# When the first group's twiddled inverse matrices are made, and which other groups are made early, in a Hyena convolution with a gated network behind it

## The chip, the core and the metric

The kernel runs on one core of one Trainium2 chip. The core has a matrix engine (PE; its weight loads are shown as PEld), a vector engine (DVE), a scalar engine (ACT), a general engine (POOL) and a queue that issues transfers (SP). Each engine works through its own instructions in the order in which they were written and waits on semaphores for the others. The metric is the time of one execution in microseconds on the device, as the median of several executions; a lower one is better.

## The reference, cut to what matters

The first part is a long convolution over 12480 positions for 4 batches and 128 channels; the second is a network with a cosine gate that is applied to every position.

```python
B, S, D = x.shape                                   # 4, 12480, 128
h_mlp = np.maximum(pos_emb @ w1, 0.0) @ w2
window = np.exp(-0.01 * np.arange(S))[:, None]
h_filt = h_mlp * window
u = x * v
Uf = np.fft.rfft(u, n=2 * S, axis=1)
Hf = np.fft.rfft(h_filt, n=2 * S, axis=0)
y = np.fft.irfft(Uf * Hf[None], n=2 * S, axis=1)[:, :S]
z = (x * y).reshape(B * S, D)                       # 49920 tokens

h = z @ w_in                                        # d_ff = 2048
out = (h * np.cos(h)) @ w_out
```

## The kernel before, in words

The Fourier transforms are written as matrix products over two factors, 96 and 120. A batch goes through five steps. `u_units` loads x and v, multiplies them and folds the product into the large tile `slots`. `f1_units` and `f2_units` are the two steps of the forward transform, and `f2_units` multiplies by the filter's transform. `i1_units` is the third transform step, the first of the inverse one: 64 pairs of channels, each with four matmuls (L476), one ACT copy (`other`, L484) and two DVE instructions (L486) that write `slots` back. `i2_units` is the last step: 30 groups of four output columns each. For a group, PE multiplies `slots` by four matrices (L501, in two halves of eight instructions), DVE multiplies the result by x (L506, `zs`), and the rows go to the DRAM tensor `zd`, from which the network reads them.

The four matrices of a group lie in a tile `tm` and depend only on the column. `make_t` makes one out of two tables, `rows` and `tw_t`. It calls `turn`, which has two forms: one ACT instruction (L291) and one DVE instruction (L293); or, given a spare tile, two ACT instructions (L291, L296) and one POOL instruction (L297). `make_group` makes the four of a group and stores them in the DRAM tensor `td` (L651). When it is called with `summed` equal to G, which is 4, all four take the second form; with G // 2, the first and third take the first form. Batches 1 to 3 load every group's matrices from `td` (L670).

For batch 0 there are two sorts of groups. Those in `SOME` are made ahead by `some_groups`, within the third step of batch 0, and loaded from `td` in the last step like those of the other batches. The others are made in the last step itself, each while the group before it is multiplied: `before(j)` in `i2_units` returns the generator of `make_group`, and `units` takes one matrix of it at a time.

`units` is the frame of all steps. It first calls `before` for the tiles that are needed at once, ahead of its first `yield`, and then hands out its work in parts, each with a price in `yield`. The network's loop asks for such parts after each of its 16 chunks of a block (`owed`), so that convolution and network are interleaved on PE in a fixed order. In batch 0 a group of the last step costs 3.5 chunks (`FIRST_STEPS`), and `inverse_units` draws the loads and products of batch 1 (`u_units`) beside it.

All of this begins after the third step of batch 0, which runs without the network. Beside its 64 pairs, `beside` draws two other generators: every 14th part, a piece of `convert_units`, which turns the network's output weights from 64-bit to 32-bit words (DVE L151, L133, L141; POOL L135, L137, L147, L156; ACT L144, L146); and every fifth other part, a step of `some_groups`. There are 24 such steps, one matrix each. What is left of either generator runs at the end of the step. As its last act, `some_groups` advances `backs[0]`, the inverse units of batch 0: that opens the pool of the last step, issues the load of x for group 0 (`xs`) and makes group 0's four matrices.

In the network, a chunk is a matmul (L737), an ACT instruction (L740), a DVE rounding (L743), a POOL subtraction (L746), an ACT sine (L751), a DVE product (L753) and a second matmul (L762). Four PSUM tiles hold the results of L737 and of the transposes.

Of the kernel before, what the change touches and what calls it, by code (L numbers as in the profile page):

```python
# [30 lines left out]
def kernel(  # L31
# [68 lines left out]
    G = BANK // D  # L100
    UA = 2
    NG = N2 // G
# [262 lines left out]
    def n2s(g):  # L365

        a = g * UA
        return [*range(a, a + UA), *range(N2 - UA - a, N2 - a)]

    def load_pairs(t, src, b, first, second):  # L370

        start = src[b, first:first + UA, :]
        nc.sync.dma_start(t[:, :, :], bass.AP(
            tensor=start.tensor, offset=start.offset,
            ap=[[N2 * D, R], [(second - first) * D, 2], [1, UA * D]]))
# [114 lines left out]
    def i2_mm(ps, t, g, part):  # L490
        for i in range(part * G // 2, (part + 1) * G // 2):
            n2 = n2s(g)[i]
            a = abs(n2 - MID) if n2 >= H else n2 + 1
            if a % H == 0:
                places = a, N2 + a
            elif n2 < H:
                places = a, N2 + H + a
            else:
                places = H + a, N2 + a
            for r, place in enumerate(places):  # L500
                nc.tensor.matmul(ps[0:R, i * D:(i + 1) * D], t[:, i, r, :],  # L501
                                 slots[0:N1, :, place, :], start=(r == 0), stop=(r == 1))

    def i2_out(pool, ps, xs, b, g):
        zs = pool.tile([R, 2, UA, D], F32, name="zs")
        nc.vector.tensor_tensor(  # L506
            zs[:, :, :, :].rearrange("p h n d -> p (h n d)"), ps[0:R, :],
            xs[:, :, :].rearrange("p h n -> p (h n)"), op=ALU.mult)
        z = zs[:, :, :, :].rearrange("p h n d -> p (h n) d")
        row = (b * NG + g) * R  # L510
        if row > 0:
            nc.sync.dma_start(zd[row:row + R, :, :], z)
        else:
            zbs[0] = z
        made[0] += 1
        yield
# [7 lines left out]
    def units(n, steps, before, mm, after, parts, ahead=2):  # L524


        for j in range(min(ahead, n)):
            for _ in before(j) or ():
                pass
        yield 0.0  # L530
        last = iter(())
        for j in range(n):
            early = iter(before(j + ahead) or () if j + ahead < n else ())
            now = None
            for i in range(parts):
                if i == 0 or 2 * i == max(parts, 2):
                    now = mm(j, now, min(i, 1))
                if i == 0 and parts == 1:
                    now = mm(j, now, 1)
                next(last, None)  # L540
                next(early, None)
                yield steps / parts
            for _ in early:
                pass
            next(last, None)
            last = after(j, now)
        for _ in last:
            pass
        yield REST

    SOME = range(2, NG, 5)
    REST = 3.0
    U_STEPS, F1_STEPS, F2_STEPS, I1_STEPS, I2_STEPS = 2.0, 0.8, 2.9, 0.8, 1.5
    FIRST_STEPS, I2U_STEPS = 3.5, 3.0
# [1 line left out]
    def u_units(b, bufs, u, engine, side="left"):  # L556

        with tc.tile_pool(name="xv", bufs=bufs, side=side) as pool:
            tiles = {}

            def before(j):
                tiles[j] = u_load(pool, bufs, b, j * UA)

            def after(j, _):
                for half in range(2):
                    u_multiply(tiles[j], half, engine(j, half))
                    yield
                if j == H // UA - 2:
                    clear_gap(u)
                u_sums(u, tiles.pop(j), j * UA)  # L570
                yield

            yield from units(H // UA, U_STEPS, before, lambda j, ps, i: None, after, 3,
                             ahead=bufs - 2)

    def f1_units(bank, u, share=0.5, evict=f1_evict):
        def mm(j, ps, i):
            if i == 0:
                ps = bank()
            f1_mm(ps, u, j, i)  # L580
            return ps

        return units(CB, F1_STEPS, lambda j: None, mm, lambda j, ps: evict(ps, j, share), 2)

    def f2_units(bank):
        with tc.tile_pool(name="there", bufs=3) as pool:
            ws, hs = {}, {}

            def before(j):
                ws[j] = pool.tile([KE, 2, N2], F32, name="w")  # L590
                nc.sync.dma_start(ws[j][:, :, :], wd[j, :, :, :])
                hs[j] = pool.tile([N2, 2, CB, 4], F32, name="h")
                nc.sync.dma_start(hs[j][:, :, :, :], hd[j, :, :, :, :])

            def mm(j, ps, i):
                if i == 0:
                    ps = bank()
                f2_mm(ps, ws[j], 2 * j, i)
                return ps

            yield from units(N1 // 2, F2_STEPS, before, mm,
                             lambda j, ps: f2_product(pool, ps, hs.pop(j), 2 * j, False), 4)
# [39 lines left out]
    def make_group(pool, g, t, summed):  # L642

        for i, n2 in enumerate(n2s(g)):
            if summed < G and i % 2 == 0:
                make_t(t[:, i, :, :], n2)
            else:
                spare = pool.tile([N1, 2, R], F32, name="spare", bufs=2)
                make_t(t[:, i, :, :], n2, spare=spare[:, :, :])
            yield  # L650
        nc.sync.dma_start(td[g, :, :, :, :], t[:, :, :, :])  # L651

    def some_groups(pool):
        for g in SOME:
            t = pool.tile([N1, G, 2, R], F32, name="some", bufs=2)
            yield from make_group(pool, g, t, G)
        next(backs[0])

    def i2_units(bank, b, bufs):

        with tc.tile_pool(name="back", bufs=2, side="left" if b else "right") as pool:
            ts, xss = {}, {}

            def before(j):
                ts[j] = pool.tile([N1, G, 2, R], F32, name="tm", bufs=bufs)
                xss[j] = pool.tile([R, 2, UA * D], F32, name="xs", bufs=bufs)
                load_pairs(xss[j], x, b, n2s(j)[0], n2s(j)[UA])
                if b == 0 and j not in SOME:
                    return make_group(pool, j, ts[j], G // 2)
                nc.sync.dma_start(ts[j][:, :, :, :], td[j, :, :, :, :])  # L670

            def mm(j, ps, i):
                if i == 0:
                    ps = bank()
                i2_mm(ps, ts[j], j, i)
                return ps

            yield from units(NG, I2_STEPS, before, mm,
                             lambda j, ps: i2_out(pool, ps, xss.pop(j), b, j),
                             4 if b == 0 else 2, ahead=bufs - 1)  # L680

    def inverse_units(bank, b):

        if b + 1 == B:
            yield from i2_units(bank, b, 3)
            return
        new = u_units(b + 1, 3, slots[0:R, :, :, :],
                      lambda j, half: nc.gpsimd if b == 0 and j % 2 > half else nc.vector,  # L690
                      side="right" if b else "left")
        parts = 4 if b == 0 else 2
        for i, steps in enumerate(i2_units(bank, b, 2)):
            if i > 2 * parts:
                for _ in range(i % parts > 0 if b == 0 else 1 + i % 2):
                    next(new, None)
            yield steps * (FIRST_STEPS if b == 0 else I2U_STEPS) / I2_STEPS
        yield from new
# [95 lines left out]
    with tc.manual_schedule():  # L794
        with tc.tile_pool(name="psum", bufs=8, space=PSUM) as psum, \
                ExitStack() as first:
            def bank():
                return psum.tile([P, BANK], F32, name="ps")
# [67 lines left out]


            backs = [inverse_units(lambda: bank(), b) for b in range(B)]

            def beside(units, pieces, more=lambda pool: iter(())):  # L870
# [28 lines left out]
            nc.vector.memset(quarter[:, :], 0.25)  # L899
            nc.sync.dma_start(w_in_sb[:, :], wind[:, :])  # L900
            beside(i1_units(bank), [(w_out_sb[:, c, :], w) for c, w in out_pieces], some_groups)

        ps_acc = ctx.enter_context(tc.tile_pool(name="ps_acc", bufs=1, space=PSUM))
# [25 lines left out]
        steps = [(n, c) for n in range(NALL) for c in range(NFC)]  # L929
# [57 lines left out]
```

## Time and profile before

| | us |
|---|---|
| median of 4 runs | 3772.33 |
| lowest and highest | 3769.38, 3773.37 |
| the profiled execution | 3773.37 |
| its span, first to last instruction | 3771.6 |
| PE busy | 3694.4 (98%) |
| DVE busy | 2781.5 (74%) |
| ACT busy | 2519.1 (67%) |
| POOL busy | 2573.4 (68%) |

The profile comes from one execution. Its page gives the busy time of each engine and, slice by slice, the share of time it was busy and the clock that PE was granted, where 1.00 is full speed. The chain of work that ended last is followed back from the last instruction, each time to what released the waiting one. A timeline gives start, duration, engine, line, and the tiles written and read; "x4" after a row counts instructions merged into it; in brackets stands how long the engine was idle before, and what ended that. A busy PE is not PE at its peak, because matmuls are pipelined and their ends are modelled.

### The profile page before, as it was taken

How to read it: one execution, taken by the hardware profiler on the slowest of the kernel's cores; microseconds unless marked ns; L12 is line 12 of the kernel's file. 1: busy time of each engine (PE TensorE's matmuls, PEld its weight loads, DVE VectorE, ACT ScalarE, POOL GpSimd, SP SyncE). 2: the span in 40 equal slices, each digit the busy share in tenths (PEclk: the TensorE clock that was granted, in tenths of full speed). 3: DMA queues.
4: the chain of work that ended last, by engine and by line, in shares of the span. 5: the costliest groups of instructions: out<-in, count | busy, mean ns of one | idle time of the engine just before them, and what ended most of it. 6: DMA issues, size and time to landing. Idle time of an engine off the chain costs nothing.

```text
span 3771.6 us, 47191 instructions
## 1 busy us (share of the span) xinstructions
PE 3694.4 (98%) x13546; PEld 2108.3 (56%) x13546; DVE 2781.5 (74%) x5562; ACT 2519.1 (67%) x4683; POOL 2573.4 (68%) x2342
## 2 busy tenths in 40 slices
PE   7898999999999999999999999999999999999999
PEld 6777555655566555555565556555566544444444
DVE  7887887688866777788766786788765566666666
ACT  5757776766665557766655567666664677777777
POOL 7667776588854665688745664788644577777776
PEclk9999999999999999999999999999999999999999
DMA  6263551022202550122103540122105200000000
GB/s 166 63 186 105 150 149 56 18 71 79 74 18 69 178 159 28 33 79 79 57 18 110 177 124 20 49 79 75 41 14 172 82 23 17 17 23 17 17 23 13
DMA packets 209498, 276.14 MB, mean 73 GB/s; under 512 B 17111, under 2 KB 146535, under 8 KB 209111
## 3 DMA queue, kind: packets, MB, share of 16 engines
q1 hardware_dynamic: 209239, 273.12, 24.6%
q8 instruction: 109, 1.79, 0.2%
q14 instruction: 150, 1.23, 0.1%
HBM read 193.64 MB, written 79.42 MB: 72 GB/s over the span
## 4 chain that ended last, share of the span: by engine, by line
PE 86%; DVE 4%; POOL 3%; DMA 3%; ACT 2%; issue 2%; SPq 0%; POOLq 0%; DVEq 0%; ACTq 0%
PE ph L737 33%; PE acc L762 28%; PE cv L501 5%; PE cv L762 5%; PE cv L476 4%; PE cv L404 3%; PE cv L445 3%; PE ph L126 2%; POOL f L746 2%; DMA hd<-h 2%; PE ps L404 1%; DMA tm<-td 1%; ACT cs L751 1%; DVE gt L753 1%; PE ps L476 1%
## 5 line engine op out<-in xcount | busy, mean ns | idle before, releaser
L746 POOL TENSOR_TENSOR f<-a,k 128x512 f32<-128x512 f32 (+1 forms) x1568 | 1989.1, 1269 | 1056.8 <-DVE k L743 1054.2
L737 PE MATMUL ph<-at,w_in_sb 128*128 128x512 f32 (+1 forms) x3136 | 1598.8, 591 | 8.3 <-DVE gt L753 7.5
L740 ACT ACTIVATE a<-ph,quarter 128x512 f32<-128x512 f32 (+1 forms) x1568 | 1072.2, 684 | 678.0 <-PE ph L737 669.3
L762 PE MATMUL acc<-gt,w_out_sb 128*128 128x512 f32 (+1 forms) x2688 | 1369.5, 591 | 0.0
L753 DVE TENSOR_TENSOR gt<-ph,cs 128x512 f32<-128x512 f32 (+1 forms) x1568 | 1077.7, 687 | 371.0 <-ACT cs L751 356.2
L751 ACT ACTIVATE cs<-f 128x512 f32<-128x512 f32 (+1 forms) x1568 | 981.2, 626 | 394.7 <-POOL f L746 392.3
L743 DVE TENSOR_SCALAR k<-a 128x512 f32<-128x512 f32 (+1 forms) x1568 | 798.3, 509 | 541.9 <-ACT a L740 530.2
L762 PEld LDWEIGHTS acc<-gt,w_out_sb 128*128 128x128 f32 x2688 | 508.0, 189 | 642.5 <-issue 631.2
L737 PEld LDWEIGHTS ph<-at,w_in_sb 128*128 128x128 f32 x3136 | 552.2, 190 | 342.8 <-issue 257.9
L471 POOL TENSOR_TENSOR slots<-slots,t 120x256 f32<-120x256 f32 x384 | 311.4, 817 | 61.9 <-DVE t L464 35.1
L501 PEld LDWEIGHTS cv<-slots,tm 96*104 96x104 f32 x1920 | 239.2, 169 | 114.4 <-issue 82.0
L501 PE MATMUL cv<-slots,tm 96*104 96x128 f32 x1920 | 254.7, 274 | 13.6 <-DMA tm<-td 5.2
L762 PE MATMUL cv<-gt,w_out_sb 128*128 128x512 f32 (+1 forms) x448 | 224.5, 583 | 0.7 <-DVE gt L753 0.7
L476 PEld LDWEIGHTS cv<-cs,slots 120*96 120x96 f32 x1536 | 176.7, 167 | 67.6 <-issue 65.5
L476 PE MATMUL cv<-cs,slots 120*96 120x120 f32 x1536 | 183.1, 266 | 0.0
L445 PE MATMUL cv<-slots,w 124*120 124x256 f32 x576 | 173.0, 380 | 0.0
L445 PEld LDWEIGHTS cv<-slots,w 124*120 124x120 f32 x576 | 103.6, 184 | 123.8 <-issue 112.3
L404 PEld LDWEIGHTS cv<-c,slots 104*124 104x124 f32 x768 | 132.5, 192 | 71.3 <-issue 58.3
L404 PE MATMUL cv<-c,slots 104*124 104x192 f32 x768 | 151.2, 326 | 4.9 <-DVE gt L753 3.6
L762 PEld LDWEIGHTS cv<-gt,w_out_sb 128*128 128x128 f32 x448 | 84.9, 190 | 104.5 <-issue 99.5
L392 DVE TENSOR_TENSOR xt<-xt,vt 104x256 f32<-104x256 f32 x177 | 134.3, 762 | 0.3 <-DMA vt<-in_v_dram 0.3
L486 DVE TENSOR_TENSOR slots<-cv,other 96x240 f32<-96x240 f32 x384 | 133.1, 394 | 1.5 <-ACT other L484 1.4
(129 smaller groups left out, 2552.2 us busy)
## 6 DMA issues: line engine op xcount, KB each, us to landing
h<-hd SPq DMA_DIRECT2D x144, 240.0 KB
tm<-td SPq DMA_DIRECT2D x96, 312.0 KB
xt<-in_x_dram SPq DMA_DIRECT2D x120, 208.0 KB
vt<-in_v_dram SPq DMA_DIRECT2D x120, 208.0 KB
xs<-in_x_dram SPq DMA_DIRECT2D x120, 208.0 KB
zd<-zs SPq DMA_DIRECT2D x119, 208.0 KB
zb<-zd SPq DMA_DIRECT2D x96, 256.0 KB
w<-wd SPq DMA_DIRECT2D x144, 116.2 KB
```

Source lines behind the costliest of these rows:

```text
L404: nc.tensor.matmul(ps[0:KE, i * 2 * N1:(i + 1) * 2 * N1], u[:, b, 0:KE, i], c1[0:u.shape[0], :, :].rearrange("p r k -> p (r k)"), start=Tr ...
L445: nc.tensor.matmul(pi, w[:, i, :], parts[0:KE, :, k], start=True, stop=True)
L471: nc.gpsimd.tensor_tensor(y[:, r], y[:, r], t[:, r], op=op)
L476: nc.tensor.matmul(ps[0:N1, (i * 2 + r) * N2:(i * 2 + r + 1) * N2], parts[0:N2, r, :, b, i], cs[:, r, :], start=True, stop=True)
L501: nc.tensor.matmul(ps[0:R, i * D:(i + 1) * D], t[:, i, r, :], slots[0:N1, :, place, :], start=(r == 0), stop=(r == 1))
L737: nc.tensor.matmul(ph[:, 0:m], w_in_sb[:, c * P:(c + 1) * P], ats[n][:, 0:m], start=True, stop=True)
L740: nc.scalar.activation(a[:, 0:m], ph[:, 0:m], AF.Identity, bias=quarter[:, 0:1], scale=INV_TWO_PI)
L743: nc.vector.tensor_scalar(out=k[:, 0:m], in0=a[:, 0:m], scalar1=ROUND, scalar2=ROUND, op0=ALU.add, op1=ALU.subtract)
L746: nc.gpsimd.tensor_tensor(f[:, 0:m], a[:, 0:m], k[:, 0:m], op=ALU.subtract)
L751: nc.scalar.activation(cs[:, 0:m], f[:, 0:m], AF.Sin, scale=TWO_PI)
L753: nc.vector.tensor_tensor(gt[:, 0:m], ph[:, 0:m], cs[:, 0:m], op=ALU.mult)
L762: nc.tensor.matmul(accs[n][:, 0:m], w_out_sb[:, c, :], gt[:, 0:m], start=(c == 0), stop=(c == NFC - 1))
```

## The change

The set `SOME` has a step of 6 instead of 5: groups 2, 8, 14, 20 and 26 are made ahead, where it was 2, 7, 12, 17, 22 and 27. The four matrices of group 0 are made one at a time as steps of `some_groups`, ahead of its last group (26), and no longer in one go behind all of them. For this `units` now yields after each matrix of what it does in advance, `some_groups` advances `backs[0]` G + 1 times, once per step, and `inverse_units` passes the four additional yields of batch 0 through. The last matrix of group 26 is then what runs at the end of the third step.

```diff
         for j in range(min(ahead, n)):
             for _ in before(j) or ():
-                pass
+                yield 0.0
         yield 0.0
...
-    SOME = range(2, NG, 5)
+    SOME = range(2, NG, 6)
...
     def some_groups(pool):
         for g in SOME:
+            if g == SOME[-1]:
+                for _ in range(G + 1):
+                    next(backs[0])
+                    yield
             t = pool.tile([N1, G, 2, R], F32, name="some", bufs=2)
             yield from make_group(pool, g, t, G)
-        next(backs[0])
...
         parts = 4 if b == 0 else 2
-        for i, steps in enumerate(i2_units(bank, b, 2)):
+        back = i2_units(bank, b, 2)
+        for _ in range(0 if b else G):
+            yield next(back)
+        for i, steps in enumerate(back):
             if i > 2 * parts:
```

## The prediction

> **What bounds the kernel now.** I read the page's busy rows first: PE is busy 98% of the span, and its slices leave room only in the first sixth. Three stretches bound the question: the third step with its tail (273.4 to 338.5 us), the first inverse pass beside the network (to 600), and the rest.
>
> ```profile
> 273.40:338.50 65.10, 56.03 (x512) 54.59 (x512) 49.66 (x154) 42.65 (x132) 45.31 (x59) 0.96 0.25 78
> 338.50:600.00 261.50, 247.63 (x965) 141.15 (x966) 224.91 (x363) 188.65 (x378) 197.81 (x197) 0.99 0.50 148
> 600.00:3771.60 3171.60, 3156.79 (x10892) 1720.51 (x10890) 2282.45 (x4446) 2124.33 (x3674) 2144.11 (x1816) 1.00 0.21 62
> ```
>
> The columns are stretch, length, busy time of PE, weight loads, DVE, ACT, POOL, then clock, DMA share, GB/s. From 600 us on PE has 15 us free in 3172, and the change alters no instruction there. A microsecond won or lost before 600 therefore reaches the end whole. Before 600, PE waits about 14 us in the first pass, so that stretch is not PE's alone.
>
> Next, the chain that ended last, at the tail of the third step:
>
> ```profile
> 336.91 0.33 DVE power L151
> 337.24 0.20 DVE slots L486
> 337.48 1.02 DVE slots L486 x3
> 338.50 0.35 DVE tm L293
> 338.86 0.04 issue
> 338.90 3.76 PE cv L501 x16
> 342.68 0.70 DVE zs L506
> ```
>
> The third step ends with the last L486 at 338.50. Of group 0's matrices only the first DVE instruction (L293, 0.35) is on the chain; then come 16 matmuls, 0.235 us each. Are they slow because the other matrices are late? The fine stretches say no:
>
> ```profile
> 336.00:337.00 1.00, 0.00 (x0) 0.00 (x0) 1.00 (x4) 1.00 (x4) 0.08 (x1) 0.83 0.00 0
> 337.00:338.00 1.00, 0.00 (x0) 0.00 (x0) 1.00 (x4) 1.00 (x4) 1.00 (x2) 0.50 0.00 0
> 342.00:343.00 1.00, 1.00 (x7) 1.00 (x6) 0.32 (x1) 0.00 (x0) 0.39 (x1) 0.50 0.73 232
> 344.00:345.00 1.00, 0.41 (x5) 0.21 (x3) 0.00 (x0) 0.51 (x1) 0.00 (x0) 1.00 0.58 155
> ```
>
> PE has nothing to do from 334 on, its granted clock is 0.50 from 337 to 343, and in 342 to 343 it is busy throughout at that clock. The last matrix of group 0 is made by 340.24 (POOL L297, 339.62 plus 0.62), two microseconds before the 16 end. The clock sets their pace.
>
> Then the price of a group made within the first pass. The timeline of L506, one per group, gives the time from group to group; these are groups 10 to 17:
>
> ```profile
> 424.63 0.68 DVE L506 TENSOR_TENSOR zs<-cv,xs 104x512 f32<-104x512 f32 x1
> 431.59 0.68 DVE L506 TENSOR_TENSOR zs<-cv,xs 104x512 f32<-104x512 f32 x1
> 441.22 0.67 DVE L506 TENSOR_TENSOR zs<-cv,xs 104x512 f32<-104x512 f32 x1
> 449.11 0.68 DVE L506 TENSOR_TENSOR zs<-cv,xs 104x512 f32<-104x512 f32 x1
> 458.98 0.68 DVE L506 TENSOR_TENSOR zs<-cv,xs 104x512 f32<-104x512 f32 x1
> 466.95 0.68 DVE L506 TENSOR_TENSOR zs<-cv,xs 104x512 f32<-104x512 f32 x1
> 475.69 0.68 DVE L506 TENSOR_TENSOR zs<-cv,xs 104x512 f32<-104x512 f32 x1
> 483.31 0.68 DVE L506 TENSOR_TENSOR zs<-cv,xs 104x512 f32<-104x512 f32 x1
> ```
>
> Two groups without a loaded one (from 12 to 14) take 17.76, elsewhere in the pass up to 17.84. The pair around the loaded group 12 (424.63 to 441.22) takes 16.59, the pair around 17 (466.95 to 483.31) 16.36. A group that is loaded and not made saves 1.2 to 1.5 us there.
>
> **The change part by part.**
>
> **Other groups kept.** Groups 2, 7, 12, 17, 22, 27 become 2, 8, 14, 20, 26. Group 2 is common. Pair sums over all 30 of L506 give what the old five save against 17.83: 7: 1.32, 12: 1.23, 17: 1.48, 22: 1.25, 27: 1.49, together 6.77. The four new ones are all even, like 12 and 22, so 4 x 1.24 = 4.96. Cost: 6.77 - 4.96 = +1.81 us. Why are the even ones worth less? PE's weight loads wait 2.2 us for the loaded matrices at group 12 and 1.5 at 22, but 0.3 and 0.2 at 17 and 27. Bounds: if the new ones saved as odd ones do (1.48 each), +0.85; if their loads ate the whole saving, +6.8. I take +1.81, since even rows exist. In instructions this is one group more: six ACT (0.45 each), two DVE L293 (median 0.97), two POOL L297 (0.8) and one store on SP, one load of 312 KB less.
>
> **The tail.** Old: six ACT, two DVE, two POOL, a load of xs and a store of td stand between the third step and the first L501. New: the last matrix of group 26 (two ACT, one POOL) and its store, which L501 does not need. DVE loses L293 in front, so PE starts after the last L486, at 338.54 for 338.90: -0.36 us. The 16 matmuls keep 3.76, since PE is idle from 334 to 338.5 still. Bounds: 0, and -2.0 if the clock were full (16 x 0.13 = 2.1 for 3.76, with the 0.36). The load of group 2's matrices (issued 343.83, landed 348.27) meets a freer queue, as xs and one store have gone earlier. That is worth nothing: the network's fourth up-projection waits until 349.4 for the first gate (L753 at 348.79, 0.59), since PSUM holds four of L737's results, and that gate moves only with the start.
>
> **Within the third step.** Of 24 places, 23 still make a matrix and one issues a store alone. Matrices 1 and 3 of group 0 take one ACT instruction and one DVE instruction (L293) where one of another group takes two ACT and a POOL. ACT and POOL have gaps here, so what they save (0.37 of ACT at a place) counts for no more than the DVE gap behind it, 0.21 to 0.25. DVE carries the step: it runs L486 back to back between conversions. So L293's time counts. Undisturbed it is 0.42. But beside POOL it is longer:
>
> ```profile
> 419.12 0.73 POOL L392 TENSOR_TENSOR xt<-xt,vt 104x256 f32<-104x256 f32 x1
> 419.70 1.61 DVE L293 SCALAR_TENSOR_TENSOR tm<-rows,tw_t,tm 96x208 f32<-96x208 f32 x1
> 419.81 1.27 POOL L746 TENSOR_TENSOR f<-a,k 128x512 f32<-128x512 f32 x1
> ```
>
> It ends 0.23 after two POOL instructions that follow without a gap. The L486 rows, which read a matmul's result, keep 0.36 whatever POOL does. By the built order, the first L293 comes behind the third unit after a conversion: 320.5 in old times, with POOL at L147 to 320.73 and L297 behind it without a gap to about 321.3. It ends near 321.55: 1.05, less the DVE gap of 0.21 that it fills, +0.84. The second comes behind the first unit after the next conversion, at 325.91. POOL then runs L137 (325.84 to 326.92), and L147 follows with a gap of 0.07. It ends near 327.16: 1.25, less gaps of 0.25 and 0.21, +0.8. Together +1.6. Bounds: +0.2 (0.42 each, less the gaps) and +2.4 (held through L147 as well, to 327.96). I take +1.6, as the three rows above show both the hold and its end. The place that only stores saves nothing: no DVE gap stands behind it (L486 at 328.34 runs without one until L151 at 330.25).
>
> On SP, the xs load and td store of group 0 move ahead of group 26's store. The conversion's loads are already issued, and the store's wait for POOL holds up only that later store. The two L293 hold L486 and so ACT's next copy of a result, both within the sum above; PE has up to eight banks ahead and no one waits for it.
>
> The rule in the Trainium skill, "SBUF — State Buffer", section "Who interferes with whom", speaks against the move: a DVE instruction with two SBUF inputs contends with a GpSimd one that reads SBUF, and whichever starts later blocks until the other's whole instruction is done. Read as one instruction, it would free the first L293 at the end of L147 (0.47 in all, +0.26) and the second at the end of L137 (+0.8): +1.1. The 1.61 us row shows the hold lasting over two instructions without a gap, which makes +1.6.
>
> **Sum:** +1.81 - 0.36 + 1.6 = +3.05 us against the profiled execution's 3773.37 (span 3771.6, and 1.8 around it), so 3776.4. That execution stands 1.04 above the median of 3772.33; on the median it is 3775.4, +0.08%. What this kernel's measurement can tell from no change is about 0.2%, 7.5 us.
>
> **The rivals.**
>
> **The tail was the point (faster).** L293 is not held, the clock returns early and the new groups save as odd ones: +0.2 - 2.0 + 0.85 = -0.95 us, 3771.4. For it: 7 us of half clock stand there. Against it: PE's idle stretch stays over 4 us. Chance 0.15; even so not faster by 0.2%.
>
> **Loads come late (slower).** In the first pass the even groups' matrices are read soon after the load is issued, and PE waits. The load of group 2 takes 4.43 us from issue to landing. If each of the four waits another 2.2 us (the worst wait seen), the exchange costs 1.81 + 8.8, and the total is +11.9: 3784.2. For it: 2.2 and 1.5 at both even groups. Against it: those waits are already in the 1.24. It passes 7.5 us from 1.1 us more at each of the four. Chance 0.10.
>
> **The hold is longer, or absent.** DVE is held through all of POOL's conversion (+2.4), or not at all (+0.2), the rest as forecast: 3776.2 or 3774.0. Chance 0.25. **The exchange costs nothing**, because other waits fill in: 3773.6. Chance 0.05.
>
> **How the numbers follow.** The forecast itself has 0.45; all but the late loads are within 0.2%. The low end is the first rival less the 2 us by which runs of before scatter; the high end is the largest bound of the exchange with the largest hold, +8.8 us: 3769.5 to 3781. Faster by over 0.2%: 0.03, out of the first rival's 0.15, for a return of the clock that does more than I priced; slower: 0.11, the late loads and 0.01 of the longer hold; within: the other 0.86.
>
> **What would show it.** Right: two L293 of about 1 us within the third step; its last L486 1 to 2 us later; the first L501 directly behind it; clock still 0.50 there; pairs around 7, 12, 17, 22, 27 at 17.8 and around 8, 14, 20, 26 at 16.6; identical durations after 600. Wrong: L293 at 0.42, a full clock at the first L501, or pairs that stay long around the new groups.

## The result, and the profile after

| | before | after |
|---|---|---|
| median of the runs shown, us | 3772.72 (61 runs) | 3776.88 (41 runs) |
| lowest and highest, us | 3769.38, 3777.64 | 3772.14, 3784.19 |
| after by before, with its 95% interval | | 1.0012 [1.0008, 1.0016] |
| the profiled execution, us | 3773.37 | 3780.25 |
| its span, us | 3771.6 | 3778.5 |

The change costs 4.2 us (0.11% of the medians). That is slower, within the 0.2% that the prediction calls no change. The forecast was +3.05 us. The runs scatter over 12 us where those of before scatter over 8, and the profiled execution lies 3.4 us above its own median, so its trace shows more loss than the median has.

I read the same three stretches first (stretch, length, busy time of PE, weight loads, DVE, ACT, POOL, then clock, DMA share, GB/s):

```profile
273.40:338.50 65.10, 55.58 (x508) 54.30 (x507) 51.00 (x155) 42.95 (x131) 43.90 (x56) 0.95 0.26 81
338.50:600.00 261.50, 243.73 (x944) 137.95 (x944) 218.88 (x353) 182.86 (x367) 191.84 (x192) 0.98 0.48 143
600.00:3778.50 3178.50, 3163.18 (x10907) 1723.41 (x10905) 2292.81 (x4453) 2121.95 (x3682) 2149.13 (x1820) 1.00 0.21 62
```

The middle row is the one that moved: PE is busy 243.73 where it was 247.63, and its clock is 0.98 where it was 0.99. To place the loss I measured from event to event, since this execution also reaches the third step 2.6 us earlier, with nothing changed before it:

| stretch, us | before | after | difference |
|---|---|---|---|
| start to the third step's first L476 | 273.42 | 270.80 | -2.62 |
| from there to the first L501 | 65.48 | 65.86 | +0.38 |
| first L501 to the first L506 | 3.78 | 3.75 | -0.03 |
| first L506 to the thirtieth | 243.87 | 252.53 | +8.66 |
| thirtieth L506 to the end | 3185.04 | 3185.54 | +0.50 |

Nearly all of it is in the first inverse pass. The timeline of L506, one row per group, here groups 6 to 8 and 18 to 21:

```profile
387.99 0.67 DVE L506 TENSOR_TENSOR zs<-cv,xs 104x512 f32<-104x512 f32 x1
394.86 0.68 DVE L506 TENSOR_TENSOR zs<-cv,xs 104x512 f32<-104x512 f32 x1
407.06 0.68 DVE L506 TENSOR_TENSOR zs<-cv,xs 104x512 f32<-104x512 f32 x1
...
494.93 0.68 DVE L506 TENSOR_TENSOR zs<-cv,xs 104x512 f32<-104x512 f32 x1
501.88 0.68 DVE L506 TENSOR_TENSOR zs<-cv,xs 104x512 f32<-104x512 f32 x1
515.45 0.67 DVE L506 TENSOR_TENSOR zs<-cv,xs 104x512 f32<-104x512 f32 x1
523.32 0.68 DVE L506 TENSOR_TENSOR zs<-cv,xs 104x512 f32<-104x512 f32 x1
```

The pair around the loaded group 8 (387.99 to 407.06) takes 19.06 and that around 20 (494.93 to 515.45) takes 20.52, where the forecast had 16.6 and a pair without a loaded group takes 17.85. These two loads not only save nothing, they cost. The pairs around 14 and 26 took 16.38 and 17.05. Of the groups that lost their load, 12, 17 and 22 behaved as forecast: the pairs around them took 17.93, 17.85 and 17.76. Groups 7 and 27 now stand beside a loaded one, so their pairs do not show it.

What happens at group 20 is seen on PE's timeline (start, duration, engine, line; in brackets, idle before):

```profile
497.55 1.02 PE L768 MATMUL acc<-gt,w_out_sb 128*128 128x512 f32 x2
501.74 2.01 PE L501 MATMUL cv<-slots,tm 96*104 96x128 f32 x8 [3.16 <-DMA tm<-td]
503.54 1.91 PE L743 MATMUL ph<-at,w_in_sb 128*128 128x512 f32 x2
```

The timeline of the queue SP over the same stretch:

```profile
492.38 0.39 SPq L727 DMA_DIRECT2D zb<-zd  x1
494.42 0.33 SPq L651 DMA_DIRECT2D td<-tm  x1
495.64 0.32 SPq L373 DMA_DIRECT2D xs<-in_x_dram  x1
496.05 0.34 SPq L673 DMA_DIRECT2D tm<-td  x1
```

The load of the group's matrices (L673; L670 before) is issued at 496.05, and PE, which reads it next, starts 5.7 us later, after an idle wait of 3.16. Then the matmuls themselves are slow: two of L743 take 1.91 where two of the same shape (L768) took 1.02. PE's own stretches (length, busy, clock, DMA share, GB/s) show why:

```profile
498.00:501.00 3.00, 0.57 (x2) 1.00 0.79 268
501.00:507.50 6.50, 5.76 (x13) 0.50 0.42 121
507.50:512.00 4.50, 4.50 (x20) 0.97 0.00 0
```

From 501.0 on the granted clock is 0.50, for 6.83 us. In 6.50 us of these PE is busy for 5.76, so a wait of 3.2 us is followed by about 2.9 us of lost matmul time. At group 8 a wait of 2.12 is followed by 3.41 us at 0.50. Before has no half clock between 345 and 600.

The waits of PE and its weight loads in 345 to 600 for loaded matrices (total, times, longest, us), before:

```profile
PEld cv L501 <- DMA tm<-td: 5.1, 5, 2.2
...
PE cv L501 <- DMA tm<-td: 2.6, 2, 1.4
```

After:

```profile
PE cv L501 <- DMA tm<-td: 7.6, 4, 3.2
PEld cv L501 <- DMA tm<-td: 7.1, 4, 3.0
```

In the third step, DVE and POOL around the two L293 of group 0:

```profile
317.35 0.73 POOL L147 TENSOR_TENSOR sig<-sig,low 128x256 f32<-128x256 f32 x1
317.83 0.47 DVE L293 SCALAR_TENSOR_TENSOR tm<-rows,tw_t,tm 96x208 f32<-96x208 f32 x1
318.04 0.76 POOL L297 TENSOR_TENSOR some<-some,spare 96x208 f32<-96x208 f32 x1
...
323.57 1.08 POOL L137 TENSOR_SCALAR power<-power 128x256 uint32<-128x256 uint32 x1
323.61 0.58 DVE L293 SCALAR_TENSOR_TENSOR tm<-rows,tw_t,tm 96x208 f32<-96x208 f32 x1
```

They take 0.47 and 0.58, not 1.05 and 1.25. The first began beside L147 and ended at 318.30, long before L297 did at 318.80. The second ran inside L137 and was not held to its end at 324.65.

Last, the chain at the tail of the third step:

```profile
334.91 0.33 DVE power L151
335.24 1.27 DVE slots L486 x4
336.52 0.14 issue
336.65 4.75 PE cv L501 x24
```

And the fine stretches there (columns as in the first fence):

```profile
336.00:337.00 1.00, 0.35 (x2) 0.38 (x3) 1.00 (x3) 1.00 (x4) 1.00 (x2) 0.50 0.00 0
337.00:338.00 1.00, 1.00 (x6) 1.00 (x6) 0.65 (x2) 1.00 (x4) 0.62 (x1) 0.50 0.27 76
```

L293 is gone from the chain, and the first L501 starts 0.14 after the last L486, where it was 0.40. The clock is still 0.50, for 6.83 us as before.

### The profile page after: what moved, and what is told of

It is laid out like the page before. It is cut to its first block, busy times and chain, and to the rows that moved or that the text cites. A ratio compares the mean times of both kernels' runs of the same rounds, so it can differ in the third digit from the quotient of the medians.

```text
span 3778.5 us, 47191 instructions
## 1 busy us (share of the span) xinstructions
PE 3696.6 (98%) x13546; PEld 2108.2 (56%) x13546; DVE 2786.3 (74%) x5564; ACT 2511.6 (66%) x4681; POOL 2573.1 (68%) x2340
## 4 chain that ended last, share of the span: by engine, by line
PE 86%; POOL 3%; DMA 3%; DVE 3%; ACT 2%; issue 2%; SPq 0%; POOLq 0%; DVEq 0%; ACTq 0%
PE ph L743 33%; PE acc L768 28%; PE cv L501 5%; PE cv L768 5%; PE cv L476 4%; PE cv L445 3%; PE cv L404 3%; PE ph L126 2%; POOL f L752 2%; DMA hd<-h 2%; DMA tm<-td 1%; PE ps L404 1%; PE ps L476 1%; ACT cs L757 1%; DVE slots L486 0%
## 5 line engine op out<-in xcount | busy, mean ns | idle before, releaser
L743 PE MATMUL ph<-at,w_in_sb 128*128 128x512 f32 (+1 forms) x3136 | 1601.0, 592 | 8.5 <-DVE gt L759 7.6
L768 PE MATMUL acc<-gt,w_out_sb 128*128 128x512 f32 (+1 forms) x2688 | 1371.3, 592 | 0.0
L749 DVE TENSOR_SCALAR k<-a 128x512 f32<-128x512 f32 (+1 forms) x1568 | 809.2, 516 | 543.4 <-ACT a L746 528.2
L768 PEld LDWEIGHTS acc<-gt,w_out_sb 128*128 128x128 f32 x2688 | 508.6, 189 | 643.8 <-issue 632.0
L743 PEld LDWEIGHTS ph<-at,w_in_sb 128*128 128x128 f32 x3136 | 552.8, 190 | 343.5 <-issue 251.9
L501 PEld LDWEIGHTS cv<-slots,tm 96*104 96x104 f32 x1920 | 239.5, 170 | 118.9 <-issue 83.5
L501 PE MATMUL cv<-slots,tm 96*104 96x128 f32 x1920 | 255.2, 275 | 18.1 <-DMA tm<-td 10.5
L768 PE MATMUL cv<-gt,w_out_sb 128*128 128x512 f32 (+1 forms) x448 | 224.5, 583 | 0.7 <-DVE gt L759 0.7
L476 PEld LDWEIGHTS cv<-cs,slots 120*96 120x96 f32 x1536 | 176.7, 167 | 67.6 <-issue 65.5
L476 PE MATMUL cv<-cs,slots 120*96 120x120 f32 x1536 | 183.1, 266 | 0.0
L768 PEld LDWEIGHTS cv<-gt,w_out_sb 128*128 128x128 f32 x448 | 84.9, 190 | 104.5 <-issue 99.5
L486 DVE TENSOR_TENSOR slots<-cv,other 96x240 f32<-96x240 f32 x384 | 133.1, 394 | 1.5 <-ACT other L484 1.4
```

The costliest lines, as they stand in the source:

```text
L476: nc.tensor.matmul(ps[0:N1, (i * 2 + r) * N2:(i * 2 + r + 1) * N2], parts[0:N2, r, :, b, i], cs[:, r, :], start=True, stop=True)
L743: nc.tensor.matmul(ph[:, 0:m], w_in_sb[:, c * P:(c + 1) * P], ats[n][:, 0:m], start=True, stop=True)
L749: nc.vector.tensor_scalar(out=k[:, 0:m], in0=a[:, 0:m], scalar1=ROUND, scalar2=ROUND, op0=ALU.add, op1=ALU.subtract)
L768: nc.tensor.matmul(accs[n][:, 0:m], w_out_sb[:, c, :], gt[:, 0:m], start=(c == 0), stop=(c == NFC - 1))
```

## The experiments

Three theories were set against each other. A: the loads of the new groups land late, because those groups are even. B: one group more is made in the pass, and that is the whole price. C: the price is in the place of group 0's matrices (held L293, a tail that gives nothing). Each experiment was timed in eleven runs beside runs of before on the same chip. Diffs are against the changed kernel unless said otherwise.

| experiment | median, us | by before |
|---|---|---|
| e1_exchange | 3776.94 | 1.0012 [1.0003, 1.0021] |
| e2_place | 3774.00 | 1.0004 [0.9995, 1.0013] |
| e3_odd | 3773.15 | 0.9999 [0.9990, 1.0008] |
| e4_swap | 3773.75 | 1.0003 [0.9994, 1.0011] |
| e5_no_l293 | 3776.16 | 1.0008 [0.9999, 1.0017] |
| e6_before_swap | 3772.03 | 0.9996 [0.9987, 1.0005] |
| e8_double | 3781.53 | 1.0019 [1.0010, 1.0028] |
| e7_all | 3773.62 | 0.9997 [0.9988, 1.0006] |
| e9_fill20 | 3773.51 | 0.9990 [0.9981, 0.9999] |
| e10_seven | 3773.91 | 0.9990 [0.9981, 0.9999] |
| e11_nine | 3771.46 | 0.9989 [0.9980, 0.9997] |
| e12_change_fill | 3778.43 | 1.0005 [0.9996, 1.0014] |

Before had a median of 3773.09 on the chip of the first four, 3773.18 on that of the next four, and 3775.54 on that of the last four.

### The two halves of the change

The exchange of groups alone, with group 0 behind them as before (against before):

```diff
-    SOME = range(2, NG, 5)
+    SOME = range(2, NG, 6)
...
             yield from make_group(pool, g, t, G)
+        for _ in range(G):
+            yield
         next(backs[0])
```

> Groups 2, 8, 14, 20, 26 ahead as in the change, but group 0's matrices stay in one go at the end of the third step, where they were before; the four places that this leaves empty in the third step come after the five groups. If the loss lies in the first inverse pass, because the even groups' loads land late and PE's clock falls behind the wait (theory A), or because one group more is made there whatever its number (theory B), this run keeps it: +4 us against before, within 1.5. If the loss lies in the third step, where DVE's L293 is held beside POOL (theory C), it is gone: -0.5 to +1.

The placement alone, with six groups as before:

```diff
-    SOME = range(2, NG, 6)
+    SOME = range(2, NG, 5)
```

> Six groups ahead as before (2, 7, 12, 17, 22, 27), with group 0's matrices one at a time in front of the last of them. Its 24 places no longer hold all, so group 27's four matrices are made at the end of the third step, where the first matmuls of the last step do not need them. Theories A and B: 0 to +1 us against before (the trace of the changed kernel has +0.4 from the start of the third step to the first L501). Theory C: +3 or more.

The exchange alone costs 3.85 us and the placement alone 0.9, with an interval that includes no cost and also the 3 us of theory C. What speaks against C is the exchange, which has nearly the whole loss without the new place, and the trace of the placement: from the third step's first matmul to the first L501 it takes 66.07, only 0.6 more than before. In the exchange's trace the first pass is 3.5 us longer than before, with more waiting for loads than before (2.6 and 5.1), if less than in the whole change:

```profile
PEld cv L501 <- DMA tm<-td: 6.3, 4, 2.6
...
PE cv L501 <- DMA tm<-td: 5.1, 4, 2.1
```

The pairs around 8, 14 and 20 take 16.40, 16.39 and 16.73 there, and that around 26 takes 18.52, with the half clock for 3.41 us after a wait of 1.74. At 20 PE waited 2.07 and the clock did not fall. So in this trace a wait alone cost little, and a wait after which the clock fell cost about 2 us (18.52 - 16.39 = 2.1).

The placement's trace shows that the old groups are not free of this either. Its groups are those of before, and there group 12 waited 2.22 us, the clock stood at 0.50 for 3.41 us, and the pair around it took 18.47; in the trace of before the wait was 1.40 and the pair 16.59. Group 22 waited 0.68 there, for 1.25. The waits differ from one execution to the next.

### Late loads: other groups, another order of issue, twice the load

Odd groups, as many as in the change:

```diff
-    SOME = range(2, NG, 6)
+    SOME = (2, 7, 13, 19, 25)
```

> The change with groups 2, 7, 13, 19, 25 ahead: five as in the change, the same number made in the last step, but odd ones behind the first. Theory A: odd groups' loads have about a microsecond more and PE hardly waits for them, so the exchange costs 1.0 us and the whole +1.5 against before, 3 us less than the change; no half clock between 345 and 600. Theory B: the same as the change, +4.2. Theory C: the same as the change.

The even groups of the change, with their load issued before the load of xs instead of behind it:

```diff
+                made_here = b == 0 and j not in SOME
+                if b == 0 and j in SOME:
+                    nc.sync.dma_start(ts[j][:, :, :, :], td[j, :, :, :, :])
...
-                if b == 0 and j not in SOME:
+                if made_here:
                     return make_group(pool, j, ts[j], G // 2)
-                nc.sync.dma_start(ts[j][:, :, :, :], td[j, :, :, :, :])
+                if b > 0:
+                    nc.sync.dma_start(ts[j][:, :, :, :], td[j, :, :, :, :])
```

> The change, with the load of a loaded group's matrices issued ahead of the load of x for the same group, in batch 0 alone. That load of x waits for the product two groups back to free its buffer; the matrices' own buffer is free about a microsecond sooner. Theory A: the four even loads land about 1 us sooner, PE's waits shrink from 2 to 3 us to 1 to 2, the clock stays full, and the kernel gains 2 to 3.5 us on the change: +1 to +2 against before. Theories B and C: the same as the change, +4.2.

Both are back at the time of before within the noise, each with one group fewer made ahead than before has. The intervals against before are wide, but the runs on the same chip are apart: ten of the eleven with odd groups and seven of the eleven with the other order are faster than the fastest of the exchange alone (3774.42). Their waits for loaded matrices in 345 to 600, with odd groups:

```profile
PEld cv L501 <- DMA tm<-td: 2.3, 3, 1.7
...
PE cv L501 <- DMA tm<-td: 0.9, 1, 0.9
```

The same view with the other order of issue:

```profile
PE cv L501 <- DMA tm<-td: 0.3, 1, 0.3
```

Neither trace has a half clock between 345 and 600. With the other order the even group 20 saves what it should; its pair, from group 18 to group 20, takes 16.47 where it took 20.52. So it is not the even number that costs, but when the load goes out:

```profile
492.76 0.68 DVE L506 TENSOR_TENSOR zs<-cv,xs 104x512 f32<-104x512 f32 x1
499.72 0.68 DVE L506 TENSOR_TENSOR zs<-cv,xs 104x512 f32<-104x512 f32 x1
509.23 0.68 DVE L506 TENSOR_TENSOR zs<-cv,xs 104x512 f32<-104x512 f32 x1
```

The first pass takes 244.61 with odd groups and 245.12 with the other order, for 243.87 before: +0.7 and +1.25. That is the price of one group more without late loads, as single traces show it. By these figures B is a fifth to a third of the exchange's 3.85, and A the rest.

The counter-test makes the loads late where they were not: odd groups, each load issued twice.

```diff
-                nc.sync.dma_start(ts[j][:, :, :, :], td[j, :, :, :, :])
+                for _ in range(2 if b == 0 else 1):
+                    nc.sync.dma_start(ts[j][:, :, :, :], td[j, :, :, :, :])
```

> The kernel with groups 2, 7, 13, 19, 25 ahead, with each of these loads issued twice in batch 0, so that the matrices land a transfer later (312 KB more in the queue, some 1.5 to 3 us). Theory A: PE then waits at the odd groups too, 1 to 4 us each, and its clock falls behind some of the waits: +6 to +20 us against before, where one load each gave +0.1. Theory B: as with one load, 0 to +1.

It costs 8.35 us over before, where odd groups with one load cost 0.06. The computation is the same; the wait for the loads has grown:

```profile
PEld cv L501 <- DMA tm<-td: 10.9, 4, 4.0
PE cv L501 <- DMA tm<-td: 10.6, 5, 3.2
```

PE's other waits in 345 to 600 did not grow (10.6 us with one load, 7.7 with two). Of the 9.7 us more of waiting, 5.6 reach the length of the pass (250.22 for 244.61), with one half clock of 3.41 us. A stands. The same order of issue in the kernel before, with its six groups, three of which (2, 12 and 22) are even (against before; the second half of the edit is that shown above):

```diff
+                made_here = b == 0 and j not in SOME
+                if b == 0 and j in SOME:
+                    nc.sync.dma_start(ts[j][:, :, :, :], td[j, :, :, :, :])
```

> The kernel before, with the loaded groups' matrices ahead of the load of x in batch 0. Theory A: the waits at groups 12 and 22 (1.4 and 1.25 us of PE in the trace of before) go, and with them a fall of the clock in some executions: 0.5 to 2 us faster than before, and a smaller scatter. Theory B: no change.

The pass is only 0.37 us shorter, and the median, 1.15 lower, is not clearly other than before's. Between these two traces, two waits of 1.25 to 1.4 us that drop no clock were worth next to nothing.

### The L293 in the third step

Group 0's matrices are made by ACT and POOL alone:

```diff
-                    return make_group(pool, j, ts[j], G // 2)
+                    return make_group(pool, j, ts[j], G // 2 if j else G)
```

> The change, with all four matrices of group 0 made by two ACT instructions and one POOL instruction, so that no L293 stands in the third step. The prediction's term (L293 held 1.05 and 1.25 us) would give a third step 1.6 us shorter than that of the changed kernel; the rows of the changed kernel (0.47 and 0.58) give 0.4 to 0.6 shorter. In the whole time: +3.6 to +4 against before by the rows, +2.6 by the prediction's term.

From the step's first matmul to the first L501 it takes 65.29, for 65.86 with the change: the two L293 cost 0.57 us, not 1.6. The median, +3.0 against before, lies between the two forecasts and can't tell them apart; it is the trace that does. The kernel is still late, so the larger part of the loss is elsewhere: in this trace too the clock falls behind the waits at groups 8 and 20, and the pass takes 251.33. Without L293 the stretch is 0.19 shorter than before's 65.48, near the 0.26 that the shorter tail saves.

### The half clock at the tail

Matmuls whose results nobody reads were put behind the third step, to keep PE at work until the first L501. With 28 calls, odd groups, early loads and no L293 in the third step:

```diff
+            warm = bank()
+            for _ in range(28):
+                nc.tensor.matmul(warm[0:N2, 0:N2], cs[:, 0, :], cs[:, 1, :],
+                                 start=True, stop=True)
```

> Groups 2, 7, 13, 19, 25 ahead; the load of the matrices ahead of that of x; no L293 in the third step; and 28 additional matmuls of two tables, whose result nobody reads, on PE between the third step's last matmul and the first L501, where PE is idle for 4.5 us. If the half clock at the first 16 L501 comes from that idle time, they take 2.1 us for 3.76. In all 1 to 2.5 us faster than before. If the clock is low for another reason, the 16 keep 3.76 and the whole is 0 to +1.

The clock stays at full and the first L506 comes 2.03 us after the first L501, not 3.75. But the 56 instructions ran for 6.04 us and held that first L501 back by 1.8 (67.09 for 65.29), so nothing was won, where 1 to 2.5 us were expected. With 20 calls, all else alike:

```diff
-            for _ in range(28):
+            for _ in range(20):
```

> As the run with everything together, with 20 additional matmuls instead of 28. There they ran 6.0 us and held back the first L501 by 1.8 us; 20 should end about 4.3 us after the third step's last matmul, ahead of the last L486. If the clock stays full, the first L501 starts where it did without them, the 16 take 2.1 us, and the kernel is 1.5 to 2.5 us faster than before. If it falls again, 0 to -0.5.

Now they end before they are in the way (PE's timeline):

```profile
334.63 4.36 PE L914 MATMUL ps<-cs 120*120 120x120 f32 x40
339.42 2.88 PE L501 MATMUL cv<-slots,tm 96*104 96x128 f32 x24 [0.43 <-DVE slots L486]
342.20 0.58 PE L126 MATMUL ph<-ident,zs 104*128 104x104 f32 x4
```

The 24 of L501 take 2.88 where they took 4.75 with the change. The first L501 comes at 65.26 and the first L506 2.03 later: 1.97 us less than before from the start of the step to that L506, against 1.0 more in the first pass for the group given up. The ratio to before is 0.9990, its interval just below 1: against before a gain of about 2 us, a small one, and on one chip.

The change as it was, with the same 20 calls:

```diff
+            warm = bank()
+            for _ in range(20):
+                nc.tensor.matmul(warm[0:N2, 0:N2], cs[:, 0, :], cs[:, 1, :],
+                                 start=True, stop=True)
```

> The change itself with the 20 additional matmuls between the third step and the first L501, nothing else. If the half clock there costs what the 16 matmuls show (3.75 against 2.0), the kernel is 1.5 to 2 us faster than the change, +2.3 to +2.7 against before; the late loads at groups 8, 14, 20, 26 stay.

The tail wins its 1.72 us again (2.03 for 3.75). The late loads stay, with two half-clock stretches of 3.41 us in the pass, and its median remains above before's (3778.43 for 3775.54), though the interval includes no difference. On that chip it lies 4.9 us above the version with odd groups, early loads and no L293.

### More groups made ahead

The price of making a matrix ahead in the third step against what a loaded group saves: with e9's kernel, seven and nine odd groups, a matrix at every third part of the step instead of every fifth.

```diff
-    SOME = (2, 7, 13, 19, 25)
+    SOME = (3, 7, 11, 15, 19, 23, 27)
...
-                        elif i % 5 == 0:
+                        elif i % every == 0:
...
-            beside(i1_units(bank), [(w_out_sb[:, c, :], w) for c, w in out_pieces], some_groups)
+            beside(i1_units(bank), [(w_out_sb[:, c, :], w) for c, w in out_pieces], some_groups, 3)
```

> The same with seven odd groups ahead (3, 7, 11, 15, 19, 23, 27) and a place for a matrix at every third part of the third step instead of every fifth. A group made ahead saves 1.5 us in the first inverse pass and lengthens the third step by 0.5 (the run with groups 2, 8, 14, 20, 26 and the old place of group 0 had four matrices fewer there and was 0.5 shorter). Theory A: 2 to 3 us faster than five groups, 3.5 to 5 faster than before. If the third step has no room for more (ACT as its bound), 0 to 1 slower than five groups.

```diff
-    SOME = (3, 7, 11, 15, 19, 23, 27)
+    SOME = (3, 5, 9, 11, 15, 17, 21, 23, 27)
```

> The same with nine odd groups ahead (3, 5, 9, 11, 15, 17, 21, 23, 27). Theory A, if ACT still has room: 4 to 5 us faster than five groups, 5 to 7 faster than before. If neighbours' loads (two groups apart) crowd the queue or ACT is full, no better than seven.

With seven, the first L501 comes 5.0 us later in the step than with five, 0.6 for each of the eight matrices added, and the pass is 3.4 shorter. With nine it comes 6.5 later, 0.4 for each of sixteen, and the pass is 6.05 shorter. By the traces that is a loss of 1.6 and of 0.5; by the medians seven equals five, and nine has the lowest time of all, 3771.46, with an interval that overlaps e9's. Both miss their forecasts, 2 to 3 and 4 to 5 us faster than five: a matrix added cost more in the third step (0.4 to 0.6 us) than the 0.13 that was put in, 0.5 for the four of a group. Whether nine is better than five is not settled here.

## Why the prediction was right in its number and half wrong in its terms

**Other groups kept (+1.81; bounds +0.85 and +6.8).** The direction was right and the size was off, because a mechanism was left out: the fall of the clock. Without late loads the exchange costs 0.7 with odd groups, close to the lower bound, and 1.25 with even ones. With the order of issue as it is, it costs 3.85 in the median (the exchange alone, within the bounds) and 8.7 in the pass of the profiled execution, beyond the upper bound. The step that failed is "I take +1.81, since even rows exist". The rows of groups 12 and 22 held waits of 1.4 and 1.25 us on PE after which the clock stayed, and I priced the new groups as two rows of that kind repeated. The waits at 8, 20 and 26 were 2.12, 3.16 and 1.65, and two of them took the clock along. A wait's cost has a step in it, the clock, and two rows below the step do not show it (the last section has where the step lies). They came from one execution, too: with the same groups in the placement's trace, group 12 lost its clock.

**The rival "loads come late" (+11.9 by 2.2 us more at each of four).** This was the thing that happened, in part: waits at two or three of four, 4.2 us in the median. Its argument against, "those waits are already in the 1.24", held for group 14 only. Two of the prediction's own signs of being wrong came: an L293 near 0.42, and pairs that stay long around new groups (8 and 20).

**The tail (-0.36).** Measured -0.26: L501 follows the last L486 by 0.14 instead of 0.40. That the half clock stays, with 3.75 for 3.76, was right, and the versions with matmuls in the gap show that it was the clock and not the other matrices that set the pace of those 16: at full clock they take 2.03, where the bound had 2.1.

**Within the third step (+1.6; bounds +0.2 and +2.4).** Measured +0.57 (against the version without L293) to +0.64 (0.38 and the 0.26 of the tail). The failed step is "the hold lasting over two instructions without a gap": the 1.61 us row of L293 was taken for the rule. Here L293 got its turn between L147 and L297, which took 0.76 itself, and was not held through L137 at all. This is no accident of one execution: in the traces of e3, e4, e8 and e12, which have the same two instructions in the same places, they take 0.47 and 0.58 or 0.59.

The Trainium skill, "SBUF — State Buffer", section "Who interferes with whom", says that the one of the two engines that comes later is blocked for the other's whole instruction. Read as one instruction it gave 0.47 for the first L293, and 0.47 was measured; for the second it would have held L293 to the end of L137 at 324.65, and the trace shows 0.58, over at 324.19. There the measurement goes against the page.

**The sum.** +3.05 was forecast and +4.2 measured. A term too high by 1.0 met a term too low by 2.0. That the sum came so near was luck. That durations after 600 us stay the same was right: from the last group's L506 to the end, all the traces have 3184.4 to 3186.9, which is scatter between executions.

## What to carry to other kernels

When a load is moved to another place in a loop, compare the time from its issue to its first use in that place, what stands in front of it in its queue included; a saving read off other places holds only where that time is the same. Here a wait on PE well under 1.7 us was nearly free, while longer ones could cost 2 to 4 us by way of the clock (pairs of 18.52 and 20.52 for 16.4), so put the clock's fall into the upper bound of a new wait's price, and read waits off more than one execution. Where PE must stand still for some microseconds before a dense stretch, matmuls without a use can keep its clock up, as long as they end before the work arrives.

## What the runs showed of the hardware that was not expected

The clock did not follow the length of a wait: it fell after 2.12 and 3.16 us (the change, groups 8 and 20) and after 1.74 (the exchange alone, group 26), and not after 1.65 (the change, group 26) or 2.07 (the exchange, group 20). What it follows came out when all fourteen traces were laid side by side. Within one trace, before the last microseconds, the times at which the clock falls all lie on one grid of 3.413 us: in the change's trace 272.29, 333.73, 395.17 and 500.99, which are 18, 18 and 31 steps apart to within 0.02 us. The grid lies elsewhere in nearly every execution. Counting PE's idle time in each cell of its grid:

| wait, us | trace, group | most idle time in one cell, us | clock at the cell's end |
|---|---|---|---|
| 1.40 | before, 12 | 1.09 | stays |
| 2.12 | the change, 8 | 2.12 | falls |
| 3.16 | the change, 20 | 2.41 | falls |
| 1.65 | the change, 26 | 1.48 | stays |
| 2.07 | the exchange, 20 | 1.66 | stays |
| 1.74 | the exchange, 26 | 1.74 | falls |

Over the fourteen traces, without their first 25 and last 12 us, the clock fell from full to half 75 times, each time at the end of a cell with at least 1.68 us idle, which is about half of the cell. Of 181 cells with 0.9 us idle or more after which it stayed at full, all but two had less than 1.68 (the two have 1.95 and 1.96, and nothing here says why they stayed). So in these traces a wait under 1.68 us in an otherwise busy stretch left the clock alone. One of 3.4 must fill half of some cell, so by this reading it costs the clock, the two exceptions aside. Between them the place of the grid would decide, which differs from execution to execution. This was read off after the runs; no run was made to test it, and what decides whether the half clock then lasts 3.41 us or 6.83 stays open.

The Trainium skill, "TensorE: Matmul & The Clock Gate", section "What's actually happening", describes a free-running window of 3413 ns, which is the grid seen here, and says that the clock goes cold after at least one idle window. On the second point the traces differ: half a window of idle time was enough.

The wider scatter goes with it, though no run shows that this is its cause. Over the executions of the changed kernel, those with a mean clock of 0.993 or 0.994 over the span (20 of 42) took 3779.5 us on average and those with 0.995 or 0.996 took 3775.6. Of before, on the three chips of the experiments, 31 of 99 were at 0.993 or 0.994, with 3776.2, and the others took 3773.4. The lower clock comes more often with the change.

Why the loads at groups 8 and 20 take 5.0 and 5.7 us from issue to PE's start, where those of 12 and 22 took 4.2 and 4.4 before, stays open. A store of td goes out 1.6 us ahead of the load at group 20, but so it did at 12 and 22 before. A load of zb 3.7 us ahead is new at group 20, but group 8 has none. And the figure moves between executions: 3.6 at group 8 with the exchange alone, 5.0 at group 12 with the placement alone.
